# Order of the first loads, the queue of the layer-one words, PSUM banks and waiting rules in a planned attention and two-layer feed-forward kernel

## The chip, the cores and the metric

The kernel runs on one core of one Trainium2 chip. A core has five instruction streams: TensorE (PE, matrix products, with PEld for its weight loads), VectorE (DVE), ScalarE (ACT), GpSimd (POOL) and SyncE (SP, which here only issues DMAs). The metric is device microseconds of one execution, lower is better.

## The reference

A linear recurrence over 768 steps for 4 x 8 heads of size 40 makes a sequence of tokens, and two feed-forward layers follow on all 3072 tokens.

```python
for t in range(S):                       # B, H, S, D = 4, 8, 768, 40
    y[:, :, t] = einsum('bhd,bhde->bhe', rt, state)
    Sa = einsum('bhde,bhe->bhd', state, at)
    state = state * wt - Sa bt^T + vt kt^T
x = y.transpose(0, 2, 1, 3).reshape(3072, 320)
h = x @ w_in;   x = (h * tanh(softplus(h))) @ w_out      # layer one, d_ff 2048
h = x @ w_in2;  out = (h * cos(h)) @ w_out2              # layer two, d_ff 2048
```

## The kernel before

**Attention.** The 768 steps are 24 chunks of 32, and the heads are two halves, so there are 48 steps `g` (chunk `g // 2`, half `g % 2`). `pre(g)` loads a step's inputs into `IN` (two buffers, and a piece of `TMP` for `g = 1`), scans the decay (L559 to L565), makes `AM` and `KB` (L573, L579), multiplies them on TensorE (`g1`, L596), masks the product (L606) and stores it to `l_d`. `inverse` reads two steps' products back into `XM`, solves 28 small VectorE instructions one after the other (L668, L666), stores `t_d` and loads it as `TT`; `halves` (L705 to L713) ends the inverse. `chain(g)` carries the state: L776, L790, L822 or L799, L848, L874, L918 on TensorE, with evictions on ACT and VectorE between them (L389, L858, L885), and writes `Y` (L893). When four steps are done their `Y` goes to `x_d`.

**Feed-forward.** `layer1(blk)` takes one of 12 blocks of 256 tokens. It loads `XR`, splits it in a rounded part `XH` (ACT, L1032) and a rest `XL` (DVE, L1034), and runs eight groups: `h_tasks` (L977, 16 matmuls), two Mish activations (L1047, L1049), `GL` (L1052), `outs` (L958, 12 matmuls). A block can begin when the chain has made its four steps. `layer2` does the same with a cosine, mostly on blocks of 512 tokens (L992, L1008), after all of layer one's attention buffers are free (`switch`).

**Weights.** `prep` loads 64-bit words of 512 columns (`RW` or `RL` buffers), and turns each into a rounded part and a rest: Prelu on ACT (L458), a shift and an or on DVE (L463, L468), a copy `hi` on ACT or DVE (L389, L391), a subtraction `lo` on POOL (L497). Layer one's words are converted during the first chunks, layer two's after the chain has ended. Prelu and Mish are in different activation tables.

**The order.** Every piece of work is a `Task` of a `Plan`. `Plan.run` walks through modelled time: on each engine it picks the task that can start first, with small ties broken by `prio`, and so fixes the order of instructions on every engine when the kernel is built. Chain tasks have the lowest `prio` numbers (first), then `pre` and `inverse`, layer one's words, layer one, layer two. A DMA task is taken to land `lat` us after its issue (`DMA_LAT` is 3.0). Small matmuls use parts of the array (`MODE`); a group that would change TensorE from full to part use is held for up to `AGE` = 8 us, to go with others. PSUM has eight banks: four in ring `PA` for the attention, two in `PH` and two in `PO` for the feed-forward.

The built program has one thing that is not in the Python text: the landing of each DMA is told by one of eight semaphores `DMAHW0` to `DMAHW7`, which the DMAs of all queues are given in turn. A DMA therefore waits on its queue until the one that last had its semaphore has landed.

## Time and profile before

| | |
|---|---|
| three runs | 1154.07, 1154.3, 1161.89 us (median 1154.3) |
| profiled execution | 1154.66 us |
| span of its trace | 1153.0 us, so 1.66 us lie outside the trace |
| busy: PE, PEld | 1025.2 us (89%), 935.7 us (81%) |
| busy: DVE, ACT, POOL | 805.2 us (70%), 599.3 us (52%), 221.5 us (19%) |

The span is that from the first to the last instruction. Busy shares are averages over very different stages: the attention with layer one's words, attention with layer one, layer one with layer two's words, and layer two. The stages are to be read apart.

### The profile page before, as it was taken

The page shows a single profiled execution, that of the slowest core. Times are in us where ns is not written, and L with a number is a line of the kernel's source. Part 1 is how long each engine was busy: PE and PEld are TensorE (multiplying, and loading weights), DVE is VectorE, ACT ScalarE, POOL GpSimd, SP SyncE. Part 2 cuts the span into 40 slices and gives each one's busy share as a digit, 9 for nine tenths or more (in the row PEclk, how much of TensorE's full clock was granted, in tenths as well). Part 3 has the DMA queues.
Part 4 walks back from the last instruction along what each step waited for, and adds up shares of the span by engine and source line. Part 5 has one row for each costly group of instructions (what it writes and reads, how often), then busy time and mean ns, then how long its engine had stood idle before and what let it go on. Part 6 is the DMA issues. An engine that isn't in the chain of part 4 may idle for free.

```text
span 1153.0 us, 36365 instructions
## 1 busy us (share of the span) xinstructions
PE 1025.2 (89%) x14888; PEld 935.7 (81%) x14888; DVE 805.2 (70%) x2212; ACT 599.3 (52%) x1403; POOL 221.5 (19%) x278
## 2 busy tenths in 40 slices
PE   2265889999999999999998998889999999999997
PEld 1254678888888888989888898778999898999996
DVE  8898987897879779687677833535755655555553
ACT  3344595556455366455454646996533534343433
POOL 4223110000000000000000000333433333333333
PEclk9999999999999999989899999999999999999999
DMA  8553752554444436353552424342120101010001
GB/s 228 148 155 102 199 149 82 142 143 120 126 129 122 122 87 191 74 146 76 148 152 72 126 68 142 115 149 62 42 61 14 34 18 37 15 31 7 16 8 24
DMA packets 109366, 111.88 MB, mean 97 GB/s; under 512 B 64144, under 2 KB 88720, under 8 KB 109200
## 3 DMA queue, kind: packets, MB, share of 16 engines
q1 hardware_dynamic: 109200, 109.57, 35.0%
q8 instruction: 117, 1.92, 0.7%
q14 instruction: 49, 0.40, 0.1%
HBM read 91.43 MB, written 18.09 MB: 95 GB/s over the span
## 4 chain that ended last, share of the span: by engine, by line
PE 53%; DVE 14%; ACT 7%; issue 5%; DMA 3%; SPq 2%; POOL 0%; DVEq 0%; ACTq 0%; POOLq 0%
PE bank L992 12%; PE bank L1008 11%; PE bank L958 11%; PE bank L977 9%; DVE SV L885 2%; DVE FR L858 1%; DVE AM L606 1%; DVE XM L666 1%; DVE XT L668 1%; ACT L1047 1%; ACT L458 1%; PE bank L874 1%; PE bank L596 1%; DVE Y L893 1%; DVE GL L1052 1%
## 5 line engine op out<-in xcount | busy, mean ns | idle before, releaser
L1135 POOL TENSOR_TENSOR GL<-H,GH 128x512 fp32r<-128x512 f32 x96 | 124.2, 1298 | 215.4 <-ACT GH L1133 212.2
L389 ACT ACTIVATE FL<-bank 40x160 f32<-40x160 f32 (+1 forms) x375 | 101.2, 295 | 117.4 <-PE bank L629 60.0
L1126 ACT ACTIVATE T<-T,half_pi 128x512 f32<-128x512 f32 x96 | 69.4, 723 | 120.4 <-DVE T L1123 120.3
L1119 DVE TENSOR_SCALAR T<-bank 128x512 f32<-128x512 f32 x96 | 66.2, 689 | 91.2 <-PE bank L992 81.0
L1052 DVE TENSOR_TENSOR GL<-H,GH 128x512 fp32r<-128x512 f32 x96 | 66.8, 696 | 64.6 <-ACT GH L1049 63.7
L587 POOL MEMSET AM<- 64x256 f32 x96 | 29.3, 305 | 400.6 <-issue 308.4
L977 PE MATMUL bank<-XH,wih 128*128 128x256 f32 x448 | 95.0, 294 | 0.8 <-ACT GH L1049 0.8
L1128 DVE TENSOR_TENSOR H<-bank,T 128x512 f32<-128x512 f32 x96 | 65.9, 687 | 42.2 <-ACT T L1126 41.4
L1047 ACT ACTIVATE H<-bank 128x512 f32<-128x512 f32 x96 | 57.4, 598 | 68.1 <-PE bank L977 67.1
L1133 ACT ACTIVATE GH<-H 128x512 fp32r<-128x512 f32 x96 | 60.6, 632 | 60.4 <-DVE H L1128 57.3
L977 PE MATMUL bank<-XL,wih 128*128 128x256 f32 x448 | 89.7, 282 | 0.0
L977 PE MATMUL bank<-XH,wil 128*128 128x256 f32 x448 | 89.2, 281 | 0.0
L596 PE MATMUL bank<-AM,KB 104*64 104x64 f32 x768 | 37.5, 248 | 48.9 <-DVE KB L579 41.9
L668 DVE TENSOR_TENSOR XT<-XM 64x26 f32<-64x26 f32 (+6 forms) x336 | 67.9, 202 | 16.2 <-DMA XM<-l_d 8.1
L874 PE MATMUL bank<-FR,FL 104*64 104x72 f32 x1536 | 64.4, 241 | 12.9 <-issue 6.1
L666 DVE TENSOR_TENSOR XM<-XM,XT 64x26 f32<-64x26 f32 (+6 forms) x336 | 68.9, 205 | 8.2
L596 PEld LDWEIGHTS bank<-AM,KB 104*64 104x64 f32 x768 | 31.0, 157 | 52.7 <-issue 44.2
L874 PEld LDWEIGHTS bank<-FR,FL 104*64 104x64 f32 x1536 | 57.0, 147 | 19.7 <-issue 6.5
L977 PEld LDWEIGHTS bank<-XH,wih 128*128 128x128 f32 x448 | 69.9, 191 | 3.2 <-ACT GH L1049 1.3
L958 PE MATMUL bank<-woh1a,GH 128*128 128x320 f32 x192 | 65.3, 340 | 7.9 <-ACT GH L1049 7.8
L606 DVE TENSOR_TENSOR AM<-bank,maskG 64x128 f32<-64x128 f32 x192 | 55.1, 287 | 24.7 <-PE bank L596 18.6
L977 PEld LDWEIGHTS bank<-XL,wih 128*128 128x128 f32 x448 | 69.6, 192 | 0.0
(168 smaller groups left out, 2985.9 us busy)
## 6 DMA issues: line engine op xcount, KB each, us to landing
VR<-in_vR_dram SPq DMA_DIRECT2D x96, 160.0 KB
IN<-in_inT_dram SPq DMA_DIRECT2D x94, 161.4 KB
FR<-in_rI_dram SPq DMA_DIRECT2D x48, 180.0 KB
...
```

Of the source, the lines that this page charges most:

```text
L389: A.activation(o, i, AF.Copy)
L596: PE.matmul(gp[c0:c0 + 64, q // 2], kb()[:, q].rearrange("p a t -> p (a t)"), am()[0:104, :, q], start=True, stop=True)
L666: V.tensor_tensor(out=b[:, 0:i, i + 1:16], in0=b[:, 0:i, i + 1:16], in1=tv, op=ALU.add)
L668: V.tensor_tensor(out=tv, in0=bc(b[:, i:i + 1, i + 1:16], (2 * n, i, w)), in1=bc(b[:, 0:i, i:i + 1], (2 * n, i, w)), op=ALU.mult)
L874: PE.matmul(fp[64 * p:64 * p + 64, qp], fl()[0:104, n * D:n * D + 64], fr()[:, n], start=True, stop=True)
L958: PE.matmul(o, l[:, f, tsl], r, start=(first and f == 0 and i == 0), stop=(last and f == 1 and i == 2))
L977: PE.matmul(hp[:, f], pss[i][0], pss[i][1], start=(i == 0), stop=(i == 7))
L992: PE.matmul(bank[P.at((key, "h"))][:, 0:512], pss[i][0], pss[i][1], start=(i == 0), stop=(i == 7))
L1008: PE.matmul(o, l, r, start=(ft == 0 and i == 0), stop=(ft == NFF - 1 and i == 2))
L1052: gl = P.add(GLE, (dve(512),), lambda eng, Hv=Hv, key=key: EN[eng].tensor_tensor(out=GL_t[P.at((key, "gl"))], in0=Hv(), in1=GH_t[P.at((key ...
L1126: c = P.add("ACT", act(512, False, 1), lambda f=f, Tv=Tv: A.activation(Tv(f), Tv(f), AF.Sin, scale=-TWO_PI, bias=half_pi), preds=[b], aset ...
L1135: gl = P.add("POOL", pool(512), lambda f=f, Hv=Hv, key=key: G.tensor_tensor(out=GL_t[P.at((key, "gl"))], in0=Hv(f), in1=GH_t[P.at((key, "g ...
```

## The change

Five things change, all in what the planner is told or in who does a task.

1. `pre(g)` is entered before `load_step(g)`, the input loads of the first three steps get the lowest `prio` of all, and the rows 40 to 63 of `IN` are no longer set by DVE (`setup_in`, six memsets) but loaded from a new input `pad`. Loads of `r` and `v` wait for the scan of their step (first chunk) or for the loads of two steps before.
2. Layer one's words are issued on ScalarE's queue instead of SP's, with at most 3 instead of 6 under way (`AHEAD_W`).
3. DMA tasks carry their size `kb`: on SP's queue they land one after the other at 180 kB a microsecond plus 2 us, on ScalarE's after their own size at 100 kB a microsecond plus 2 us.
4. All eight PSUM banks are in `PA` until the first block's four steps are done; then two each are given to `PH` and `PO`.
5. `AGE` is 3 instead of 8; the `hi` copies of layer two's words go to DVE alone (`HIE2`); the second batch's inverse gets the priority pull that the first had (`PULL_INV`); the split of the first block's input has a chain's priority (`prx`).

```diff
-PULL, PULL_INV, PULL_CH = 0.3, -5000.0, -1e6
+PULL, PULL_INV, PULL_CH = 0.3, -4980.0, -1e6
...
-AGE = 8.0
+AGE = 3.0
 WAIT = 8.0
 SP_SAFE = 1.0
+RATE, RATE2, LAND = 180.0, 100.0, 2.0
+ACT_SAFE = 2.0
...
-                        st = max(st, (h[0][0] if n == 1 else sorted(h)[n - 1][0]) + (SP_SAFE if e == "SP" else 0.0))
+                        st = max(st, (h[0][0] if n == 1 else sorted(h)[n - 1][0]) + (SP_SAFE if e == "SP" else ACT_SAFE if ring in ("RW", "RL") else 0.0))
...
+            lat = t.lat
+            if t.kb and e == "ACT":
+                lat = t.kb / RATE2 + LAND
+            elif t.kb:
+                queue = max(queue, free[e]) + t.kb / RATE
+                lat = queue + LAND - free[e]
...
-                 ("PA", 4), ("PH", 2), ("PO", 2)):
+                 ("PA", 8), ("PH", 0), ("PO", 0)):
         P.ring(n, k)
-
-    def setup_in(i):
-        t = IN1 if i == 2 else IN_t[i]
-        V.memset(t[32:64, 0:768], 0.0)
-        V.memset(t[32:64, 768:], 1.0)
...
-    AHEAD_W = 6
+    AHEAD_W = 3
...
-    HIE2, HID2 = ("ACT", "DVE"), (act(512, False), 0.34)
+    HIE2, HID2 = ("DVE",), (0.34,)
...
-            t0 = P.add("SP", 0.5, lambda raw=raw, src=src: SP.dma_start(raw().rearrange("p n w -> p (n w)"), src),
+            t0 = P.add(*(("ACT", 0.4) if layer == 1 else ("SP", 0.5)), lambda raw=raw, src=src, q=A if layer == 1 else SP:
+                       q.dma_start(raw().rearrange("p n w -> p (n w)"), src),
...
             SP.dma_start(t[64:104], ins["inT"][hf, c, 1])
-
-        t_ld = fifo("ld", P.add("SP", 1.0, ld, preds=[S_IN[2]] if g == 1 else S_IN[0:2], acq=[] if g == 1 else [("IN", k("IN"))], lat=DMA_LAT + 1.5, prio=pr))
+            if g < 3:
+                SP.dma_start(t[40:64], ins["pad"])
+
+        t_ld = P.add("SP", 1.0, ld, acq=[] if g == 1 else [("IN", k("IN"))], kb=330, prio=pr if g > 3 else g - 1e6)
...
+        held = list(io[g - 2]) if c else [scanT[g]]
...
+        prx = -9.955e3 if blk == 0 else pr0
...
     for g in range(TOT):
+        pre(g)
         load_step(g)
-        pre(g)
...
+    for i in range(4):
+        P.add("SP", 0.0, lambda i=i: P.grow("PH" if i < 2 else "PO", [P.at(("bank", i))], P.time),
+              preds=ytask[0], acq=[("PA", ("bank", i))], lat=0.0, prio=-2e4)
```

The planned order changes on every engine. In what follows a name such as `AM1_202` is buffer 1 of `AM`; lines above L340 or so are a few numbers higher in the changed file (L453 is L456, L656 is L663, L977 is L985).

On SP, before: from the input of step 3 to the load that brings the first two products back for the first inverse (`XM<-l_d0`).

```order
L553 DMA IN0_192<-in_inT_dram 40x1033 [waits DMAHW5_49]
L554 DMA IN0_192<-in_inT_dram 40x1033 [waits DMAHW6_49]
L619 DMA l_d0_93<-AM1_202 32x8x32 [waits DMAHW7_49,DVE_49,Pool_49]
L620 DMA l_d0_93<-AM1_202 32x8x32 [waits DMAHW0_49,DVE_49,Pool_49]
L453 DMA TMP_172<-in_w_in_dram 128x1024 [waits DMAHW1_49]
L453 DMA TMP_172<-in_w_in_dram 128x1024 [waits DMAHW2_49,Activation_49]
L453 DMA TMP_172<-in_w_out_dram 128x1024 [waits DMAHW3_49,DVE_49,Activation_49]
L656 DMA XM_224<-l_d0_93 32x512 [waits DMAHW7_49,DMAHW4_49,DMAHW0_49]
```

On SP, now, the same place: the second step's product to the same load.

```order
L626 DMA l_d0_93<-AM1_202 32x8x32 [waits DMAHW7_49,DVE_49,Pool_49]
L627 DMA l_d0_93<-AM1_202 32x8x32 [waits DMAHW0_49,DVE_49,Pool_49]
L556 DMA IN1_193<-in_inT_dram 40x1033 [waits DMAHW1_49,DVE_49]
L557 DMA IN1_193<-in_inT_dram 40x1033 [waits DMAHW2_49]
L626 DMA l_d1_94<-AM2_203 32x8x32 [waits DMAHW4_49,DVE_49,Pool_49]
L627 DMA l_d1_94<-AM2_203 32x8x32 [waits DMAHW5_49,DVE_49,Pool_49]
L663 DMA XM_224<-l_d0_93 32x512 [waits DMAHW7_49,DMAHW6_49,DMAHW0_49]
```

Three words have left the place ahead of that load, and the input of step 4 stands there instead; its wait for `DMAHW1` is for a word that ScalarE issues, the last row of the next piece.

On ACT, now: the evictions of the first steps (`FL`), with the words' DMAs and conversions between them.

```order
L392 ACTIVATE FL1_209<-bank3_147 64x160 x3
L392 ACTIVATE wih1_164<-H0_177 128x512 [waits DVE_49]
L392 ACTIVATE FL2_210<-bank5_149 64x160 [waits PE_49]
L392 ACTIVATE FL2_210<-bank5_149 64x160 x3
L461 ACTIVATE H0_177<-TMP_172 128x512 [waits DMAHW0_49,Pool_49]
L456 DMA TMP_172<-in_w_out_dram 128x1024 [waits DMAHW1_49]
```

The word's DMA, which stood on SP before, now stands on ACT behind a conversion that waits for a landing and for POOL.

On TensorE, before: the last groups ahead of layer one's first matmul (`XH`, L977); `FL4` is of step 4.

```order
L596 MATMUL bank1_145<-AM2_203,KB0_217 64x64 x8
L629 MATMUL bank2_146<-ident_173,KB0_217 128x104 x4
L848 MATMUL bank3_147<-VR0_222 64x64 x8
L822 MATMUL bank0_144<-ident_173,ZS0_230 40x128 x4
L874 MATMUL bank1_145<-FR0_220,FL4_212 64x72 x8
L874 MATMUL bank2_146<-FR0_220,FL4_212 64x72 x8
L977 MATMUL bank4_148<-XH0_185,wih1_164 128x256 x2
```

On TensorE, now, the same place (L603 is L596, L985 is L977).

```order
L784 MATMUL bank6_150<-SV1_219,AM5_206 32x40 x16
L603 MATMUL bank2_146<-AM1_202,KB0_217 64x64 x8
L636 MATMUL bank4_148<-ident_173,KB0_217 128x104 x4
L985 MATMUL bank0_144<-XH0_185,wih1_164 128x256 x2
L985 MATMUL bank0_144<-XH0_185,wil1_165 128x256 x2
L985 MATMUL bank0_144<-XH0_185,wix1_166 128x256
```

Step 4's chain work has moved behind the first layer-one matmul, and the groups of the next steps' products stand directly ahead of it.

On ACT, before: the first of layer two's words (`AU<-RA`) among layer one's Mish activations (`H`, `GH`).

```order
L458 ACT_TABLE_LOAD
L458 ACTIVATE AU0_11623<-RA0_11620 128x512
L458 ACTIVATE AU1_11624<-RA1_11621 128x512
L1047 ACT_TABLE_LOAD
L1047 ACTIVATE H1_178<-bank0_144 128x512
L1049 ACTIVATE GH0_180<-bank0_144 128x512
L389 ACTIVATE wih2_11595<-AU0_11623 128x512
```

On ACT, now, the same place.

```order
L461 ACT_TABLE_LOAD
L461 ACTIVATE AU0_11412<-RA0_11409 128x512
L1056 ACT_TABLE_LOAD
L1056 ACTIVATE H1_178<-bank2_146 128x512
L1058 ACTIVATE GH0_180<-bank2_146 128x512
L1056 ACTIVATE H2_179<-bank4_148 128x512
L1058 ACTIVATE GH1_181<-bank4_148 128x512
```

The copies `wih2<-AU` have left ACT, and more Mish activations stand between two loads of a table.

## Rows read from the trace of the kernel before

**Rows 1.** Windows: length, then busy us of PE, PEld, DVE, ACT, POOL.

```profile
0.00:134.50 134.50, 61.02 (x1376) 50.95 (x1376) 119.39 (x345) 56.80 (x155) 38.36 (x78) 1.00 0.59 163
134.50:186.80 52.30, 46.62 (x850) 42.66 (x849) 43.56 (x141) 39.60 (x90) 10.50 (x20) 0.97 0.52 145
186.80:254.90 68.10, 64.14 (x1454) 57.51 (x1454) 59.77 (x206) 38.19 (x114) 3.67 (x12) 0.97 0.51 133
254.90:706.20 451.30, 428.17 (x8623) 392.40 (x8622) 339.39 (x1137) 237.32 (x681) 15.27 (x50) 0.98 0.43 114
706.20:790.00 83.80, 70.00 (x478) 65.15 (x477) 35.45 (x58) 73.65 (x104) 23.19 (x17) 0.96 0.42 133
790.00:1145.50 355.50, 355.19 (x2118) 326.99 (x2116) 207.60 (x330) 152.91 (x259) 130.49 (x101) 1.00 0.11 28
```

**Rows 2.** Timeline (start, length): XL of three blocks, and first matmuls of them.

```profile
133.17 0.95 DVE L1034 TENSOR_TENSOR XL<-XR,XH 128x768 fp32r<-128x768 f32 x1
134.54 0.79 PE L977 MATMUL bank<-XH,wih 128*128 128x256 f32 x2
...
181.29 0.96 DVE L1034 TENSOR_TENSOR XL<-XR,XH 128x768 fp32r<-128x768 f32 x1
...
186.84 0.39 PE L977 MATMUL bank<-XH,wih 128*128 128x256 f32 x2
...
239.37 0.96 DVE L1034 TENSOR_TENSOR XL<-XR,XH 128x768 fp32r<-128x768 f32 x1
...
254.93 0.39 PE L977 MATMUL bank<-XH,wih 128*128 128x256 f32 x2
255.16 0.39 PE L977 MATMUL bank<-XH,wil 128*128 128x256 f32 x2
```

**Rows 3.** Lines of DVE in 0 to 134 us: count, busy us, mean ns.

```profile
L666 DVE TENSOR_TENSOR XM<-XM,XT 64x14 f32<-64x14 f32 (+6 forms) x56 | 14.0, 250 | 1.3
L668 DVE TENSOR_TENSOR XT<-XM 64x14 f32<-64x14 f32 (+6 forms) x56 | 13.9, 248 | 3.8 <-DMA XM<-l_d 2.5
L468 DVE SCALAR_TENSOR_TENSOR H<-TMP,H 128x512 uint32<-128x512 uint32 x17 | 11.5, 678 | 0.1
...
L579 DVE TENSOR_TENSOR KB<-IN,RP 104x256 f32<-104x256 f32 x20 | 8.3, 416 | 0.2
...
L342 DVE MEMSET IN<- 32x768 f32 x2 | 1.4, 698 | 1.1 <-PEq L1318 1.0
```

**Rows 4.** Timeline of SP's DMA issues and DVE, 12 to 41 us.

```profile
12.03 0.71 DVE L559 TENSOR_TENSOR_SCAN PE<-IN,D 104x264 f32<-104x264 f32 x1
...
28.95 2.16 SPq L453 DMA_DIRECT2D TMP<-in_w_in_dram  x2
...
31.91 0.80 SPq L656 DMA_DIRECT2D XM<-l_d  x2
...
40.01 0.17 DVE L668 TENSOR_TENSOR XT<-XM 64x14 f32<-64x14 f32 x1 [2.54 <-DMA XM<-l_d]
```

**Rows 5.** DMA queues in 0 to 40 us.

```profile
DMA packets 4162, 8.96 MB, mean 224 GB/s; under 512 B 1856, under 2 KB 2112, under 8 KB 4160
```

**Rows 6.** Timeline of TensorE at a change from full to part use.

```profile
309.51 0.31 PE L958 MATMUL bank<-wol1b,GH 128*128 128x320 f32 x1
309.65 0.30 PE L958 MATMUL bank<-woh1b,GL 128*128 128x320 f32 x1
309.89 0.75 PE L705 MATMUL bank<-TA,TT 16*32 16x32 f32 x64
```

**Rows 7.** Lines of ACT in 710 to 790 us: count, busy us, mean ns.

```profile
L458 ACT ACT_TABLE_LOAD x12 | 15.4, 1283 | 0.2
L1047 ACT ACT_TABLE_LOAD x11 | 14.1, 1283 | 0.2
...
L389 ACT ACTIVATE wih<-AU 128x512 fp32r<-128x512 f32 x8 | 5.0, 631 | 1.5 <-DVE AU L468 1.4
```

**Rows 8.** Lines of PE in 710 to 790 us: busy us, mean ns, idle before.

```profile
L958 PE MATMUL bank<-woh1a,GH 128*128 128x320 f32 x32 | 11.0, 343 | 7.9 <-ACT GH L1049 7.8
```

More of the change, by code (lines that the diff above doesn't have):

```diff
@@ L50, with __init__ @@
 SLACK = {"PE": 0.02, "DVE": 0.02, "ACT": 0.02, "POOL": 0.2, "SP": 0.02}
-PULL, PULL_INV, PULL_CH = 0.3, -5000.0, -1e6
+PULL, PULL_INV, PULL_CH = 0.3, -4980.0, -1e6
 class Task:
-    __slots__ = ("eng", "dur", "fn", "preds", "acq", "rel", "aset", "lat", "prio", "end", "n_wait", "succ", "ready", "cols", "engs", "takes", "name", "durs", "bias", "ffn", "port", "mode", "soft", "pull", "mate")
-    def __init__(self, eng, dur, fn, preds=(), acq=(), rel=(), aset=None, lat=None, prio=0.0, cols=0.0, bias=BIAS, port=False):
-        self.bias = bias
+    __slots__ = ("eng", "dur", "fn", "preds", "acq", "rel", "aset", "lat", "prio", "end", "n_wait", "succ", "ready", "cols", "engs", "takes", "name", "durs", "bias", "ffn", "port", "mode", "soft", "pull", "mate", "kb")
+    def __init__(self, eng, dur, fn, preds=(), acq=(), rel=(), aset=None, lat=None, prio=0.0, cols=0.0, bias=BIAS, port=False, kb=0.0):
+        self.bias, self.kb = bias, kb
         self.ffn = cols > 0 and prio >= 0
@@ L135, in run @@
         done = 0
-        port_free = 0.0
+        port_free = queue = 0.0
         recent = []
@@ L229, in run @@
                 port_free = free[e]
-            t.end = free[e] + (0.2 if t.lat is None else t.lat)
+            lat = t.lat
[4 more added lines that the diff above has]
+                lat = queue + LAND - free[e]
+            t.end = free[e] + (0.2 if lat is None else lat)
             for key in t.rel:
@@ L238, in run @@
                 for x in u.engs:
-                    u.ready[x] = max(u.ready[x], free[e] + (HOP.get((e, x), 0.15) if t.lat is None else t.lat))
+                    u.ready[x] = max(u.ready[x], free[e] + (HOP.get((e, x), 0.15) if lat is None else lat))
                 u.n_wait -= 1
@@ L562, in pre @@
         t_sc = fifo("scan", P.add("DVE", 0.62, scan, preds=[t_ld, S_D], acq=[("PE", k("PE"))], prio=pr, port=True))
+        scanT[g] = t_sc
         def rscan():
@@ L620, in ldm @@
             SP.dma_start(ld_v[ci, 1], am()[32:64, 1])
-        ldma[g] = P.add("SP", 1.0, ldm, preds=t_gl, lat=DMA_LAT, prio=pr)
+        ldma[g] = P.add("SP", 1.0, ldm, preds=t_gl, kb=128, prio=pr)
         fl = lambda: FL_t[P.at(k("FL"))]
@@ L656, in ld @@
                 SP.dma_start(part(h), dr(l_d, h))
-        t = P.add("SP", 1.0, ld, preds=[ldma[g0 + i] for i in range(cnt)] + [S_X], acq=[("X", ("X", bt))], lat=DMA_LAT, prio=pr)
+        t = P.add("SP", 1.0, ld, preds=[ldma[g0 + i] for i in range(cnt)] + [S_X], acq=[("X", ("X", bt))], kb=140, prio=pr)
         def step(i, add):
@@ L741, in f3 @@
                 V.memset(sv[64:104, 1], 0.0)
[L743 to L745 removed]
+        t3 = P.add("SP", 1.0, f3, preds=[S_V] + held, acq=[("SV", k("SV"), 3 if c else 1)], kb=106, prio=pr)
+        t1 = P.add("SP", 1.0, f1, preds=[S_V] + held, acq=[("FR", k("FR"))], kb=331, prio=pr)
+        t2 = P.add("SP", 1.0, f2, preds=[S_V] + held, acq=[("VR", k("VR"))], kb=328, prio=pr)
         io[g] = (t1, t2, t3)
@@ L938, in yst @@
                 SP.dma_start(xv[1], yv[64:104])
-            ytask.setdefault(yb, []).append(P.add("SP", 1.0, yst, preds=yevs, rel=[ykey], lat=DMA_LAT, prio=pr))
+            ytask.setdefault(yb, []).append(P.add("SP", 1.0, yst, preds=yevs, rel=[ykey], kb=164, prio=pr))
     x2st = {}
@@ L1154, in store @@
                     SP.dma_start(out[r0:r0 + 64], OB_t[P.at(ok)][64 * i:64 * i + 64])
-            P.add("SP", 1.0, store, preds=[o], rel=[ok], lat=DMA_LAT, prio=pr0)
-    S_IN = [P.add("DVE", 1.1, lambda i=i: setup_in(i), prio=-1e6) for i in range(3)]
+            P.add("SP", 1.0, store, preds=[o], rel=[ok], kb=164, prio=pr0)
     S_D = P.add("DVE", 0.7, setup_d, prio=-9.5e5)
@@ L1210, in switch @@
             P.grow(r, range(len(STG[r])), P.time)
-        P.grow("PH", [0, 1], P.time)
-        P.grow("PO", [2, 3], P.time)
+        left = [i for _, i in P.rings["PA"]]
+        P.grow("PH", left[0:2], P.time)
+        P.grow("PO", left[2:4], P.time)
     def half2():
@@ L1265, in layouts @@
                           wp.reshape(NPART, NCH, 2, D, NQ * (C + 1)), wp[..., 0, :1]], axis=-1)
+    pad = np.zeros((64 - D, inT.shape[-1]), np.float32)
+    pad[:, 3 * NQ * C:] = 1.0
     def nlay(x):
@@ L1304, in layouts @@
     return {
-        "inT": inT, "rI": units(rI), "vF": units(vF), "vS": vS, "vR": vR,
+        "inT": inT, "pad": pad, "rI": units(rI), "vF": units(vF), "vS": vS, "vR": vR,
         "w_in": win_lay(w_in), "w_out": wout_lay(inputs["moe_w_out"]),
```

22 lines of the change are left out of this document (8 added, 14 removed).

## The prediction

> **What bounds the kernel now.** I read the windows first, since the averages of the page hide five different stages [rows 1]. Up to 134.5 us DVE is busy 119.4 us and PE 61.0: TensorE waits for what VectorE makes (scans, products, inverses, words). From 134.5 to 254.9 DVE still has 103.3 of 120.4 us, while PE has risen to 110.8. From 254.9 to 706.2 PE is busy 428.2 of 451.3 us and DVE 339.4: TensorE sets the pace. From 706.2 to 790 the chain is over, layer one goes on beside the conversion of layer two's words, and ACT is the full engine: 73.7 of 83.8 us, PE 70.0. From 790 on PE is never idle until 1145.5, and 7.5 us of output follow. So there are two places where TensorE waits and time can be had, the start and the stretch behind the chain. What is gained on another engine between 254.9 and 706.2 is worth little.
>
> Second I read where the first three blocks of layer one begin [rows 2]. `XL` of the first is ready at 134.1 and TensorE takes it at once. `XL` of the second starts at 181.3, its first matmul at 186.8. `XL` of the third is done at 240.3, but TensorE comes to it only at 254.9: there the bound has passed from DVE to PE. The third block is therefore the point at which I compare the two orders.
>
> **The change part by part. The first 250 us.** The order of DVE gives, by counting: ahead of the first `XL` stand 343 instructions before and 274 now, ahead of the second 472 and 517, ahead of the third 640 and 642. The 69 that leave the first stretch are the six memsets of `setup_in`, 17 instructions of the words, 27 of one inverse, and 19 of the steps' preparation and chain; the kinds cost 0.70 (the three longer memsets), 0.68 (an or of the words), 0.25 (an inverse's piece) and 0.42 us (a `KB`) [rows 3]. Priced by the mean of the stretch, 119.39 / 345 = 0.346 us [rows 1], they are 24 us. The 45 more ahead of the second `XL`, at 43.56 / 141 = 0.309 us [rows 1], are 14 us. The two more ahead of the third are 0.6 us. So the change brings the first block forward and pays it back before the third; what it removes for good on DVE is the memsets, about 3 us, which these counts already contain.
>
> To this come waits of DVE that the trace of before can't show. The first scan starts at 12.0 us now [rows 4]; the inputs that lead the queue let it start earlier, perhaps by 3. But the DMAs of the first 40 us move 8.96 MB at 224 GB/s [rows 5], so what leads pushes something else back. The first inverse started at 40.0 after 2.5 us of waiting for `XM<-l_d`, issued at 31.9, behind words issued from 28.95 [rows 4]. In the new order those words are gone from ahead of it, which speaks for an earlier inverse by up to 5 us. Instead the load of step 4 stands there, which shares its completion semaphore with a word that ACT issues, and that word stands on ACT behind a conversion that waits for POOL. SP's in-order queue then holds back the loads for the first inverse until the word has landed. I bound the cost of this from -5 us (words gone, no wait) to +12 us (two inverses, each 6 us late; 8.1 us is what the load took from issue to use at 40.0 [rows 4]) and take +4, nearer to the first end, because fewer words compete for the saturated DMA engines.
>
> Then the first `XL` starts at 133.2 - 24 + 4 = 113, and layer one about 1.4 us later (134.54 against 133.17 [rows 2]), 20 us earlier than before. The second `XL` starts at 181.3 + 14 + 4 = 199 and its block at about 202. Between the second and third block TensorE did 128 matmuls of L977, 96 of L958 and 660 small ones in the 68.1 us from 186.8 to 254.9. L977 follows itself by 0.115 us (255.16 - 254.93 for two) [rows 2], L958 by 0.147 (309.51 to 309.65) [rows 6]: 14.7 + 14.1 us, so the small ones took 39.3, or 0.06 each. Now 128, 84 and 320 stand there: 14.7 + 12.3 + 19.1 = 46 us. So the third block begins at 202 + 46 = 248, where `XL` (239.4 + 0.6 + 4 = 244) has just been made, 7 us earlier than 254.9. Up to that point 48 small matmuls fewer have been done, 2.9 us. Net **-4 us**, with bounds of -13 (TensorE takes the third block as soon as `XL` is made without the waits) and +5 (waits at 12).
>
> The DMA issues of layer one's words leave SP, which nothing waits for as an engine, and take some 0.4 us each on ACT; ACT is busy 56.8 of the first 134.5 us [rows 1], so this hides as long as no issue waits. Three `pad` loads of 99 kB are 0.3 MB, 1.3 us of the rate in [rows 5], inside the bound above. Eight banks instead of four cost nothing and I give them nothing: the waits of the first stretch are for DVE.
>
> **Changes of mode.** The order of TensorE goes from full to part use 161 times instead of 145 and back 162 instead of 146; changes among part uses fall from 100 to 90. One entry took 0.24 us from start to start where the matmul before took 0.14 [rows 6], so 0.1 us; 22 changes more are **+2 us**, from 0 (hidden in waits) to 4.
>
> **The middle.** When the chain ends, 112 matmuls of L977 and 78 of L958 more are still to do than before: 24 us of layer one are left for later, and the chain ends that much earlier. DVE's 339.4 us then fall into 427 instead of 451, 79% instead of 75%. Still not the bound; I add **+1 us** for more meetings, 0 to 8.
>
> **Layer two's words.** In 710 to 790 us ACT spends 29.5 us in 23 table loads, and its copies of `hi` take 0.63 us each [rows 7]; 20 of them stand in the order there, 12.6 us. They go to DVE, which is busy 35.5 of 83.8 us [rows 1], so it hides them. In the new order 22 Mish pairs instead of 16 share the stretch, with 27 table loads instead of 23. ACT's work becomes 73.7 - 12.6 + 4 x 1.28 + 6 x 1.2 + some 4 us for two more words and the outputs = 77 us, while TensorE's is 22 x (16 x 0.115 + 12 x 0.147) = 79 instead of 58. ACT no longer exceeds TensorE. PE's idle there, 83.8 - 70.0 = 13.8 us [rows 1], of which 7.9 stood before one line waiting for ACT's `GH` [rows 8], should fall to about 6: **-8 us**, bounds -14 and 0. If DVE did not hide the copies, conversions would end some 10 us later, and layer two is still far off.
>
> A table load shows 1283 ns here and 0.2 us of idle in front of twelve of them together [rows 7]. The Trainium skill (ScalarE: Activation LUTs, What ACT_TABLE_LOAD costs) gives the same 1283 ns, but adds a drain of about 1380 ns to every switch of sets. By the Trainium skill the four more would cost 10.6 us of ACT instead of 5.1 and the forecast would be some 5 us later; the rows show no such drain, so I price them by the row.
>
> **The sum.** 1154.66 - 4 + 2 + 1 - 8 = 1145.7 us, for an execution with 1.66 us outside the trace; the profiled execution is 0.4 us above the median of 1154.3, so I say 1145.5, 0.8% less.
>
> **Rivals.** (A) The start pays in full: TensorE begins layer one at about 110, 24 us earlier, and is fed from then on, because the second chunk's chain no longer waits for its inverse. The 140 small matmuls that are moved behind the start cost 8 us at 0.06, the modes 2, the words' stretch gives 10: 1154.7 - 24 + 8 + 2 - 10 = 1131. For it speaks that TensorE is idle 73 of the first 134.5 us; against it that the second and third `XL` have as much DVE work ahead as before or more.
>
> (B) Slower: the shared semaphores couple the two queues. Each word on ACT waits for a DMA of SP eight places back, and SP for words of ACT, so that evictions stand behind DMA issues and loads behind evictions. What the planner takes to be 0.4 us of issue becomes a wait of several us for ten words, and both first inverses come late. Third block 21 us later than forecast, 269: 1167. It decides from the point where the first inverse starts later than about 46 us. For it speak the order's rows and the saturated DMA [rows 5]; against it that before, too, words and loads stood in one queue with the same semaphores. The Trainium skill (DMA: Bandwidth & Descriptors, Issuing engines are not separate DMA queues) says that DMAs of ScalarE and SyncE run on the same 16 engines and interleave, so that a second queue saves issue time alone. The trace, with one queue in use, does not show two sharing.
>
> (C) The words' stretch gives nothing: Mish, Prelu and two banks still take turns, and four more table loads eat the freed copies: 1145.7 + 8 = 1154.
>
> **How the numbers follow.** Forecast 0.47, A 0.30, B 0.13, C 0.10. One per cent of 1154.3 is 11.5 us, about what a measurement of this kernel tells from no change: faster means below 1142.8, slower above 1165.8. The forecast's own spread, 1138 to 1153, puts some 0.07 below 1142.8: faster 0.37. Of B a fifth stays below 1165.8: slower 0.11. The rest is 0.52. The range of 1128 to 1163 leaves out a third of A and three quarters of B, 2 in 10.
>
> **What would show it.** Right: the first L985 near 114 us and the third block near 248; the first inverse near 40; PE idle between 115 and 200; fewer PE waits for `GH` behind the chain; 38 table loads instead of 34 in all. Wrong: a third block before 240 (A) or after 260 (B), DVE waiting long for `XM` or `IN`, ACT idle before a DMA issue, or PE idle of over 10 us behind the chain (C).

## The result, and the profile after

The changed kernel is slower: the median of its eight runs is 1166.41 us (1161.93 to 1171.01) against 1154.18 us of eight runs of the kernel before, a ratio of 1.0104 with a 95% interval of 1.0074 to 1.0135. I had forecast 1145.5 us and a range up to 1163. The profiled execution took 1165.52 us, its span is 1163.8.

The windows of the changed kernel, cut at the first matmul of the first three blocks (121.0, 226.5, 275.2), of the eleventh block (733.8), and of layer two (798.3). Columns as in [rows 1].

```profile
0.00:121.00 121.00, 45.64 (x1109) 39.59 (x1109) 87.92 (x274) 41.85 (x119) 29.18 (x67) 0.91 0.56 158
121.00:226.50 105.50, 78.80 (x1677) 70.26 (x1678) 89.56 (x271) 67.77 (x169) 22.55 (x35) 0.78 0.49 128
226.50:275.20 48.70, 45.52 (x814) 42.11 (x813) 37.19 (x138) 22.20 (x63) 1.23 (x4) 0.96 0.40 102
275.20:733.80 458.60, 432.84 (x8702) 393.04 (x8701) 358.81 (x1159) 251.63 (x701) 22.89 (x59) 0.99 0.46 124
733.80:798.30 64.50, 61.43 (x456) 58.95 (x455) 42.48 (x65) 51.91 (x71) 20.44 (x15) 1.00 0.43 128
798.30:1163.80 365.50, 357.56 (x2140) 329.83 (x2138) 205.95 (x332) 152.23 (x258) 128.00 (x99) 1.00 0.11 26
```

These are the cuts of [rows 1] except for the last: layer two's first matmul stood at 787.1 us before, and [rows 1] cut at 790.0. The stretch that compares with the one from 733.8 to 798.3 is this one of the kernel before:

```profile
706.20:787.10 80.90, 67.10 (x457) 62.26 (x456) 34.32 (x56) 70.96 (x99) 23.19 (x17) 0.96 0.43 138
```

Length less PE busy is TensorE's idle time. Up to the third block it is 75.4 + 26.7 + 3.2 = 105.3 us, against 73.5 + 5.7 + 4.0 = 83.2 in [rows 1]. In the middle it is 25.8 against 23.1. In the stretch behind the chain it is 3.1 against 13.8. So 22 us are lost at the start, 3 in the middle and 11 come back behind the chain, 14 more in all; TensorE's busy time is 3.4 us shorter (1021.8 against 1025.2), which leaves the 10.8 us by which the span is longer. By landmarks the third block is 20.3 us late (275.2 against 254.9), the eleventh 27.6 (733.8 against 706.2), layer two 11.2 (798.3 against 787.1), the end 10.8.

The timeline shows the three starts that answer to [rows 2]: the `XL` and the first matmul of each block (the third block's `XL` is there 18 us before its matmul).

```profile
120.98 0.80 PE L985 MATMUL bank<-XH,wih 128*128 128x256 f32 x2 [10.92 <-ACT XH L1041]
...
217.06 0.96 DVE L1043 TENSOR_TENSOR XL<-XR,XH 128x768 fp32r<-128x768 f32 x1
...
226.45 0.40 PE L985 MATMUL bank<-XH,wih 128*128 128x256 f32 x2
...
257.21 0.94 DVE L1043 TENSOR_TENSOR XL<-XR,XH 128x768 fp32r<-128x768 f32 x1
```

VectorE's work ahead of the first block did shrink, from 119.4 us (345 instructions) to 87.9 (274), but it waits. The waits of DVE in the first 130 us, and its timeline where these waits end:

```profile
DVE PE L564 <- DMA IN<-in_inT_dram: 11.2, 2, 6.6
DVE PE L564 <- DMA IN<-in_pad_dram: 7.8, 1, 7.8
DVE XT L675 <- DMA XM<-l_d: 3.1, 2, 1.6
```

```profile
13.47 0.71 DVE L564 TENSOR_TENSOR_SCAN PE<-IN,D 104x264 f32<-104x264 f32 x1 [7.76 <-DMA IN<-in_pad_dram]
...
41.30 0.71 DVE L564 TENSOR_TENSOR_SCAN PE<-IN,D 104x264 f32<-104x264 f32 x1 [4.55 <-DMA IN<-in_inT_dram]
...
44.99 0.17 DVE L675 TENSOR_TENSOR XT<-XM 64x14 f32<-64x14 f32 x1 [1.44 <-DMA XM<-l_d]
...
114.51 0.71 DVE L564 TENSOR_TENSOR_SCAN PE<-IN,D 104x264 f32<-104x264 f32 x1 [6.60 <-DMA IN<-in_inT_dram]
```

Before, no scan waited for `IN`; one inverse waited 2.5 us [rows 4]. Why the inputs come late is seen on SP's queue, in its longest waits (first 130 us: sum, times, longest) and its timeline.

```profile
SPq L735 <- DMA TMP<-in_w_in_dram: 10.3, 1, 10.3
SPq L626 <- DVE AM L613: 8.2, 4, 3.3
SPq L557 <- DMA TMP<-in_w_out_dram: 8.0, 1, 8.0
SPq L556 <- DVE XT L675: 7.0, 1, 7.0
SPq L556 <- DMA TMP<-in_w_out_dram: 5.6, 1, 5.6
```

```profile
20.20 0.30 SPq L556 DMA_DIRECT2D IN<-in_inT_dram  x1
28.56 0.29 SPq L557 DMA_DIRECT2D IN<-in_inT_dram  x1
...
37.20 0.30 SPq L556 DMA_DIRECT2D IN<-in_inT_dram  x1
...
94.07 0.28 SPq L741 DMA_DIRECT2D VR<-in_vR_dram  x1
104.76 0.28 SPq L735 DMA_DIRECT2D FR<-in_rI_dram  x1
...
109.14 0.37 SPq L556 DMA_DIRECT2D IN<-in_inT_dram  x1
```

An input load (L556, L557) has nothing to do with a word in `TMP`; what it waits for is the semaphore that this word's landing holds. All such waits for words add up to 46.1 us in the first 130; before they were 5.1. At 20.5 us SP stops between the two halves of one input, until a word lands at 28.5. That word was issued on ACT's queue at 25.01, as ACT's timeline shows:

```profile
13.23 0.35 ACTq L456 DMA_DIRECT2D TMP<-in_w_out_dram  x1
22.07 0.99 ACT L392 ACTIVATE FL<-bank 64x160 f32<-64x160 f32 x4 [8.18 <-PE bank L636]
25.01 0.34 ACTq L456 DMA_DIRECT2D TMP<-in_w_out_dram  x1
...
33.48 0.33 ACTq L456 DMA_DIRECT2D TMP<-in_w_out_dram  x1
```

The word of 25.01 stands behind an eviction that waited 8.2 us for TensorE, which waited for VectorE, which waited for its first input. So SP's load waits for ScalarE, and ScalarE for the loads' own consumers. This first stop alone made no scan wait: the scan of that input began at 31.47 us with no idle time before it. The next ones did. SP stood for 5.6 us (the last row of its waits) until 37.2, for a word that ACT issued at 33.48, and the scan at 41.30 waits for the input that then left at 37.20. The scan at 114.51 waits for the input issued at 109.14, after SP had stood for 10.3 us until 104.7. The DMA engines were not full meanwhile: the line that answers to [rows 5], for 0 to 40 us, has 6.82 MB instead of 8.96, and the queues' share of the 16 engines was 59% instead of 79%.

```profile
DMA packets 3370, 6.82 MB, mean 171 GB/s; under 512 B 1694, under 2 KB 1822, under 8 KB 3368
```

The first wait, 7.8 us for `pad`, is partly something else: in the first 13.5 us the words on ACT's queue (q10) moved more bytes than the inputs that lead SP's (q1); the columns are packets, MB and share of the 16 engines.

```profile
q10 hardware_dynamic: 432, 1.57, 40.2%
q1 hardware_dynamic: 369, 1.19, 30.0%
```

The Trainium skill (DMA: Bandwidth & Descriptors, Issuing engines are not separate DMA queues) says that DMAs of several issuing engines run on the same 16 engines and interleave. The two lines agree: both queues move bytes in the same stretch, and their shares add up to 70.2%.

Behind the chain the change did what it was meant to. ACT's lines from 735 to 798 us (answer to [rows 7]), and PE's line that answers to [rows 8]:

```profile
L461 ACT ACT_TABLE_LOAD x9 | 11.5, 1283 | 0.2
L1056 ACT ACT_TABLE_LOAD x9 | 11.5, 1283 | 0.2
```

```profile
L966 PE MATMUL bank<-woh1a,GH 128*128 128x320 f32 x32 | 10.1, 315 | 1.1 <-ACT GH L1058 1.0
```

No copies `wih<-AU` are left on ACT, and PE's idle at this line, nearly all of it for `GH`, has gone from 7.9 to 1.1 us. Part of the words now lies ahead of the window from 733.8: ACT's first table load for them is at 711.7 us, where it was at 710.8. From there to layer two's first matmul TensorE is idle for 4.0 of 86.6 us with 614 matmuls, where it was idle for 13.8 of 76.3 with 423. Idle ahead of nine loads of a table together is again 0.2 us, so the drain that the Trainium skill adds (ScalarE: Activation LUTs, What ACT_TABLE_LOAD costs) does not show here either.

### The profile page after: what moved, and what is told of

It reads as the page before. It is cut to its first block, busy times and chain, and to the rows that moved or that the text cites. A ratio compares the mean times of both kernels' runs of the same rounds, so it can differ in the third digit from the quotient of the medians.

```text
span 1163.8 us, 36363 instructions
## 1 busy us (share of the span) xinstructions
PE 1021.8 (88%) x14888; PEld 933.8 (80%) x14888; DVE 821.9 (71%) x2234; ACT 587.6 (50%) x1379; POOL 224.3 (19%) x278
## 4 chain that ended last, share of the span: by engine, by line
PE 62%; DVE 21%; issue 5%; DMA 5%; ACT 5%; SPq 1%; POOL 0%; DVEq 0%; ACTq 0%; POOLq 0%
PE bank L966 13%; PE bank L1000 12%; PE bank L985 12%; PE bank L1016 11%; PE bank L882 3%; DVE XM L673 3%; DVE SV L893 3%; DVE XT L675 3%; DVE AM L613 2%; PE bank L856 2%; PE bank L798 2%; DVE AM L580 1%; DVE GL L1061 1%; DVE KB L586 1%; PE bank L603 1%
## 5 line engine op out<-in xcount | busy, mean ns | idle before, releaser
L392 ACT ACTIVATE FL<-bank 64x160 f32<-64x160 f32 (+1 forms) x376 | 101.5, 295 | 127.7 <-PE bank L636 68.2
L985 PE MATMUL bank<-XH,wih 128*128 128x256 f32 x448 | 95.4, 295 | 14.2 <-ACT XH L1041 10.9
L1061 DVE TENSOR_TENSOR GL<-H,GH 128x512 fp32r<-128x512 f32 x96 | 68.7, 719 | 49.1 <-ACT GH L1058 47.7
L985 PE MATMUL bank<-XL,wih 128*128 128x256 f32 x448 | 90.2, 283 | 0.0
L985 PE MATMUL bank<-XH,wil 128*128 128x256 f32 x448 | 90.2, 283 | 0.0
L985 PEld LDWEIGHTS bank<-XH,wih 128*128 128x128 f32 x448 | 71.1, 194 | 16.3 <-ACT XH L1041 11.2
L603 PE MATMUL bank<-AM,KB 104*64 104x64 f32 x768 | 37.0, 246 | 49.1 <-DVE KB L586 41.0
L675 DVE TENSOR_TENSOR XT<-XM 64x14 f32<-64x14 f32 (+6 forms) x336 | 67.8, 202 | 14.0 <-DMA XM<-l_d 5.8
L603 PEld LDWEIGHTS bank<-AM,KB 104*64 104x64 f32 x768 | 30.6, 155 | 55.5 <-issue 42.3
L673 DVE TENSOR_TENSOR XM<-XM,XT 64x14 f32<-64x14 f32 (+6 forms) x336 | 67.7, 201 | 8.5
L985 PEld LDWEIGHTS bank<-XL,wih 128*128 128x128 f32 x448 | 70.3, 193 | 0.0
L985 PEld LDWEIGHTS bank<-XH,wil 128*128 128x128 f32 x448 | 70.2, 194 | 0.0
```

The costliest lines, as they stand in the source:

```text
L392: A.activation(o, i, AF.Copy)
L603: PE.matmul(gp[c0:c0 + 64, q // 2], kb()[:, q].rearrange("p a t -> p (a t)"), am()[0:104, :, q], start=True, stop=True)
L673: V.tensor_tensor(out=b[:, 0:i, i + 1:16], in0=b[:, 0:i, i + 1:16], in1=tv, op=ALU.add)
L675: V.tensor_tensor(out=tv, in0=bc(b[:, i:i + 1, i + 1:16], (2 * n, i, w)), in1=bc(b[:, 0:i, i:i + 1], (2 * n, i, w)), op=ALU.mult)
L985: PE.matmul(hp[:, f], pss[i][0], pss[i][1], start=(i == 0), stop=(i == 7))
L1061: gl = P.add(GLE, (dve(512),), lambda eng, Hv=Hv, key=key: EN[eng].tensor_tensor(out=GL_t[P.at((key, "gl"))], in0=Hv(), in1=GH_t[P.at((key ...
```

## The experiments

Theory 1: the landing semaphores, given in turn over two queues, couple SP's loads to ScalarE's stream. Theory 2: the words only take DMA bandwidth from the inputs. Theory 3: the order itself lacks work to cover the loads. One table first: median, median of the kernel before measured beside it, starts of the first three blocks, TensorE's idle up to the third (window length less PE busy), and SP's waits for words (in `TMP` or `RL`) in 130 us (not summed where a dash stands). Blocks and idle times are of one profiled execution each.

| kernel | us | before | blocks 1, 2, 3 | idle | SP for words |
|---|---|---|---|---|---|
| before | 1154.18 | | 134.5, 186.8, 254.9 | 83 | 5.1 |
| changed | 1166.41 | 1154.18 | 121.0, 226.5, 275.2 | 105 | 46.1 |
| a_q_sp | 1147.62 | 1154.93 | 102.7, 210.4, 259.1 | 88 | 9.3 |
| a_q_pool | 1152.02 | 1154.93 | 102.1, 213.2, 261.9 | 85 | 0 |
| b_words_act | 1167.71 | 1154.93 | 136.1, 204.8, 272.5 | 96 | 23.8 |
| b_hi_dve | 1143.70 | 1154.93 | 134.7, 186.5, 254.5 | 82 | - |
| b_hi_age3 | 1142.64 | 1153.28 | 134.8, 199.1, 264.8 | 83 | - |
| b_hi_banks8 | 1155.71 | 1153.28 | 162.6, 213.7, 264.6 | 86 | - |
| b_hi_lead | 1164.85 | 1153.28 | 121.0, 188.6, 263.8 | 86 | 5.1 |
| a_words_sp | 1156.53 | 1153.28 | 142.0, 217.0, 271.9 | 93 | 4.4 |
| a_sp_hi_both | 1161.17 | 1155.25 | 104.1, 216.0, 264.6 | 89 | - |
| a_sp_inv | 1141.37 | 1155.25 | 113.8, 190.6, 250.1 | 82 | 13.7 |
| a_sp_fill | 1157.28 | 1155.25 | 106.6, 218.5, 267.1 | 82 | - |
| a_act_inv | 1165.74 | 1151.45 | 131.1, 213.6, 273.2 | 106 | 47.7 |

**a_q_sp.** The changed kernel, its order kept, words on SP's queue.

```diff
-... q=A if layer == 1 else SP:
+... q=SP:
```

> The changed kernel with its planned order kept, and one thing undone: layer one's words are issued on SP's queue, at the places where ScalarE issued them. PE and DVE have the same rows in the same order. Theory 1 (coupling): in the changed kernel SP's input loads wait for semaphores that words on ScalarE's queue hold, 46 us of SP waits for TMP in the first 130 us against 5 before. With one queue that waits in order, these waits should fall below 15 us, DVE's waits for IN from 18.9 us to below 9, and the time to about 1153. Theory 2 (bytes): words and inputs share the same 16 DMA engines whatever queue they are on; inputs come about as late as now, the time stays within 1161 to 1168. Theory 3 (the order): too little work is left on DVE to cover the loads, the waits for IN stay near 18 us, 1163 to 1168.

Measured: 1147.62 us, ratio to before 0.9939 (0.9906 to 0.9972), 18.8 us less than the changed kernel. The windows up to the third block, and the first scan:

```profile
0.00:102.70 102.70, 45.62 (x1109) 39.59 (x1109) 87.64 (x272) 41.89 (x119) 29.20 (x67) 0.93 0.65 183
102.70:210.40 107.70, 81.11 (x1676) 71.94 (x1677) 89.63 (x272) 67.59 (x169) 22.31 (x35) 0.77 0.48 129
210.40:259.10 48.70, 44.08 (x814) 40.55 (x813) 37.19 (x138) 22.26 (x63) 1.22 (x4) 1.00 0.41 101
```

```profile
7.69 0.71 DVE L564 TENSOR_TENSOR_SCAN PE<-IN,D 104x264 f32<-104x264 f32 x1 [1.98 <-DMA IN<-in_pad_dram]
```

With the same instructions in the same order on PE and DVE, TensorE's idle ahead of the first block falls from 75.4 to 57.1 us; the next two stretches stay as they were. Theory 3 falls. Theory 1 gave 1153, the loss was larger. Of the 18.3 us, 5.8 are the first scan (7.69 instead of 13.47). The `pad` that it waits for left SP at 4.63 us in the changed kernel and at 2.76 here, and the scan followed 8.8 and 4.9 us later: 1.9 us lie ahead of the issue and 3.9 behind it. Behind it the bytes of theory 2 are the likely cause, and no run shows them alone. The rest fits the later waits of DVE: for `IN` 11.2 us there and none here, for `XM` 3.1 and 1.3.

**a_q_pool.** The same with GpSimd's queue.

```diff
-... q=A if layer == 1 else SP:
+... q=G if layer == 1 else SP:
```

> The changed kernel, same order on PE and DVE, words issued on GpSimd's queue, whose landings have semaphores of their own, so that no load of SP and no word wait for one another's semaphores. The bytes still go through the same 16 DMA engines at the same time. Theory 1 (coupling): SP no longer waits for TMP, DVE's waits for IN fall below 8 us, first block near 111, third near 260, time about 1150; GpSimd pays some 1 us an issue, which delays its subtractions little. Theory 2 (bytes): IN waits stay at 15 to 19 us, 1162 to 1168. Theory 3 (the order): also 1162 to 1168.

Measured: 1152.02 us, 0.997 (0.9946 to 0.9993); SP waits for no word, DVE's wait for `IN` is 1.7 us. Two queues did no such harm where SP waits for no landing of the other, so the later waits are theory 1's. As far as the traces show, the turn of eight semaphores is thus one of SP's and ScalarE's queues, and GpSimd's landings have others. An issue took GpSimd 0.56 us (27 of them 15.2), not the 1 us that I expected. The first words left it only at 7.0 us, so this run does not tell the first scan's 5.8 us apart.

**b_words_act.** The kernel before, words planned and issued on ScalarE.

```diff
-            t0 = P.add("SP", 0.5, lambda raw=raw, src=src: SP.dma_start(...
+            t0 = P.add(*(("ACT", 0.4) if layer == 1 else ("SP", 0.5)), lambda raw=raw, src=src, q=A if layer == 1 else SP:
+                       q.dma_start(...
```

> The kernel before with one thing of the change alone: layer one's words are issued on ScalarE's queue (still up to six under way, planned at 3 plus 1.5 us). Theory 1 (coupling): SP's loads begin to wait for words, 20 to 50 us of SP waits for TMP in the first 130 us, DVE's waits for IN or XM rise by 8 to 20 us, time 1160 to 1172. Theory 2 (bytes): within 3 us of before, 1152 to 1157, since the same bytes move at the same time. Theory 3 (the order): 1152 to 1157.

Measured: 1167.71 us, 1.0102 (1.0065 to 1.0139), inside theory 1's range, but only in part for its reason. SP waits 23.8 us for words (17.5 for those in `TMP`, 6.3 for those in `RL`), the third block is 17.6 us late and TensorE's idle up to it 12 us longer. But DVE's waits for `IN` or `XM`, expected to rise by 8 to 20 us, are 1.4 us in the first 130; it waits for `TT` instead (6.2 us in the first 230). And 14 us more idle stand in layer two (21.4 against 7.8), with a cause that no run here shows.

**a_act_inv.** The changed kernel with the second inverse pulled as before.

```diff
-PULL, PULL_INV, PULL_CH = 0.3, -4980.0, -1e6
+PULL, PULL_INV, PULL_CH = 0.3, -5000.0, -1e6
```

> The changed kernel with the pull of the second inverse as before (PULL_INV -5000) and nothing else undone: layer one's words are on ScalarE's queue. Order of PE and DVE as in the kernel of 1141.4 us, which issues the words on SP. Theory 1 (coupling, whatever the order): SP waits 25 us or more for words in the first 130 us, DVE 10 to 20 us for IN or XM, TensorE's idle up to the third block 95 us or more against 82.4, time 1153 to 1162. Rival (the coupling cost much because the second inverse stood where it did): idle up to the third block below 88 us, 1141 to 1147.

**a_sp_inv.** The same order on PE and DVE, words on SP: both diffs, this one and that of a_q_sp.

> The changed kernel with words on SP's queue, and the pull of the second inverse as before (PULL_INV -5000). First XL behind 299 DVE instructions instead of 274, second 491 instead of 517, third 665 instead of 642. Theory P (DVE pays the early first block back before the second): first block 8 us later than 102.7, second XL 8 us earlier than 200, TensorE's idle between the first two blocks falls from 26.6 us to 12 to 18 and that ahead of the first rises from 57 by as much, so that the idle up to the third block stays at 82 to 90 us and the time at 1142 to 1152. Rival (the pull is what costs the start): idle up to the third block falls to 75 us or less, below 1140.

Measured: 1165.74 us, 1.0104 (1.0066 to 1.0142), against 1141.37 us, 0.9897 (0.9848 to 0.9946). The windows up to the third block, first of a_act_inv, then of a_sp_inv:

```profile
0.00:131.10 131.10, 47.15 (x1172) 40.27 (x1172) 100.88 (x300) 46.11 (x126) 31.00 (x70) 0.85 0.54 156
131.10:213.60 82.50, 65.75 (x1256) 58.43 (x1249) 66.36 (x203) 57.54 (x141) 16.73 (x28) 0.87 0.45 125
213.60:273.20 59.60, 54.50 (x1195) 48.80 (x1194) 50.79 (x170) 31.96 (x93) 3.67 (x12) 1.00 0.49 132
```

```profile
0.00:113.80 113.80, 47.18 (x1172) 40.52 (x1173) 101.04 (x300) 46.30 (x126) 31.06 (x70) 0.83 0.63 179
113.80:190.60 76.80, 65.82 (x1255) 58.90 (x1249) 66.99 (x204) 57.39 (x141) 16.79 (x28) 0.88 0.48 134
190.60:250.10 59.50, 54.69 (x1193) 49.07 (x1193) 50.75 (x169) 31.96 (x93) 3.68 (x12) 0.99 0.49 133
```

A second order shows the same: DVE does 101 us of work in 131 us or in 114, and the queue alone is worth 24 us. Theory 1 has its waits (47.7 us of SP, 19.0 of DVE) and its idle (106); the time went above its 1162. As for the pull, theory P is right on the shift (first block 11 us later than in a_q_sp, idle between the first two blocks 11.0 instead of 26.6), but the idle up to the third also fell by 6, and the time by 6. The two intervals overlap, and 6 us are about what one execution can differ from another (a_sp_hi_both), so what the place of the second inverse costs is not settled.

**a_words_sp.** The changed kernel with the words also planned on SP (its `P.add` as in before, with `kb=n`).

> The changed kernel with the words planned and issued on SP's queue, so that the order is made for one queue; all other parts as changed. The order now has 352 DVE instructions ahead of the first XL (274 with the words on ScalarE), 520 and 641 ahead of the second and third. Theory 1 (coupling): no waits of SP for words beyond 15 us, DVE waits for IN below 6 us, time 1142 to 1150, near the 1147.6 of the kept order on one queue. Rival (the order made with the words on ScalarE was itself the gain of the start): third block at 265 or more, 1153 to 1160.

Measured: 1156.53 us, 1.0014 (0.9993 to 1.0035). SP waits 4.4 us for words, and yet the first block starts at 142.0 and the third at 271.9: the rival's numbers. So the coupling is not all of the start. An order made for two queues and run on one is 9 us better than the order that the planner makes for one.

**b_hi_dve.** The kernel before with the `hi` copies on DVE.

```diff
-    HIE2, HID2 = ("ACT", "DVE"), (act(512, False), 0.34)
+    HIE2, HID2 = ("DVE",), (0.34,)
```

> The kernel before with one thing of the change alone: the copies hi of layer two's words go to DVE and not to ScalarE. The order is the same up to the middle of the chain's time. Theory W (the copies bound the stretch): the stretch behind the chain becomes 12 to 17 us shorter, ScalarE's busy time in it falls by about 12 us, 1138 to 1143. Rival (what shortened the stretch in the changed kernel was that more of layer one's Mish pairs were left beside the words): a gain of at most 5 us, 1149 to 1155.

Measured: 1143.70 us, 0.9889 (0.9852 to 0.9926). The stretch behind the chain:

```profile
703.90:772.50 68.60, 61.75 (x457) 58.76 (x456) 48.11 (x76) 57.14 (x77) 24.99 (x17) 1.00 0.50 161
```

It is 68.6 us long instead of 80.9 (706.2 to 787.1), ACT's busy time 57.1 instead of 71.0, TensorE's idle 6.9 instead of 13.8. Theory W holds, one line alone gives 11 us.

**a_sp_hi_both.** That line undone in a_q_sp.

> The changed kernel with words on SP's queue at the planned places (1147.6 us), and the hi copies of layer two's words undone: ScalarE or DVE makes them, as before. The order is the same up to row 2422 of TensorE's 4414. Theory W (the copies on ScalarE bound the stretch behind the chain): TensorE's idle in that stretch goes from 3.1 us back to 10 to 14, time 1155 to 1162. Rival (the stretch is short because more Mish pairs share it): idle stays below 6 us, 1146 to 1151.

Measured: 1161.17 us, 1.0052 (1.0026 to 1.0078). The stretch is 75.0 us instead of 64.5, TensorE's idle in it 9.4 (a little below what W expected) instead of 3.1, most of it at the lines that wait for `GH` (the one shown, and `woh1b` with 3.8 us):

```profile
723.90:798.90 75.00, 65.58 (x457) 62.21 (x456) 31.78 (x50) 63.08 (x91) 19.28 (x15) 0.95 0.37 114
```

```profile
L966 PE MATMUL bank<-woh1a,GH 128*128 128x320 f32 x32 | 10.8, 336 | 4.3 <-ACT GH L1058 4.3
```

Theory W again. The third block of this execution is 5.5 us later than that of a_q_sp, with the same order up to there: so much one profiled execution can differ from another.

**b_hi_age3.** b_hi_dve with the shorter wait for company.

```diff
-AGE = 8.0
+AGE = 3.0
```

> The kernel before, with the hi copies on DVE (1143.7 us so far) and the shorter wait of TensorE's groups for company (AGE 3 instead of 8) as the one part added. The third XL has 695 DVE instructions ahead instead of 640, the first 343 as before. Theory M1 (shorter waits cost mode changes and stand against layer one): the stretch from the third block to the eleventh grows from 449 to 455 us or more, time 1149 to 1156. Theory M2 (neutral: what is done earlier is missing later): 1140 to 1147.

Measured: 1142.64 us, 0.9894 (0.9859 to 0.9929): M2. From the third to the eleventh block it takes 451.7 us (449.4 in b_hi_dve). The third block is 10.3 us later than in b_hi_dve, at the same idle (83 against 82), and the end is not: 3966 matmuls instead of 3681 lie ahead of it. A late block is thus a loss only where no more work was done before it (3600 in the changed kernel, 3680 in the kernel before).

**b_hi_banks8.** b_hi_dve with eight banks in `PA` until the first block.

```diff
-                 ("PA", 4), ("PH", 2), ("PO", 2)):
+                 ("PA", 8), ("PH", 0), ("PO", 0)):
...
+    for i in range(4):
+        P.add("SP", 0.0, lambda i=i: P.grow("PH" if i < 2 else "PO", [P.at(("bank", i))], P.time),
+              preds=ytask[0], acq=[("PA", ("bank", i))], lat=0.0, prio=-2e4)
...
```

> The kernel before, with the hi copies on DVE, and all eight banks in the attention's ring until the first block's steps are done. The order moves the first XL behind 450 DVE instructions instead of 343, the second behind 498 instead of 472. Theory N (banks bound nothing, the start is for DVE): the first block comes near 165, but the second near 195 and the third near 258, time 1142 to 1149. Rival (TensorE did useful layer-one work in the 30 us that are now given to the attention, and lacks it later): third block at 270 or more, 1155 or more.

Measured: 1155.71 us, 1.0025 (1.0002 to 1.0048), 12 us above b_hi_dve, as the rival said; the third block (264.6) lies between the two. What the banks are worth in the changed kernel, where `prx` brings the first block forward, no run shows.

**b_hi_lead.** b_hi_dve with the new order of the inputs.

```diff
-        load_step(g)
         pre(g)
+        load_step(g)
...
+            if g < 3:
+                SP.dma_start(t[40:64], ins["pad"])
...
-        t_ld = fifo("ld", P.add("SP", 1.0, ld, ... prio=pr))
+        t_ld = P.add("SP", 1.0, ld, ... prio=pr if g > 3 else g - 1e6)
...
+        held = list(io[g - 2]) if c else [scanT[g]]
...
```

> The kernel before, with the hi copies on DVE, and of the start only the new order of the inputs: input loads of the first steps lead, the rows 40 to 63 of IN are loaded from pad, loads of r and v are held back; the words stay on SP's queue and nothing waits for ScalarE. First XL behind 305 DVE instructions instead of 343, second 456 instead of 472, third 659 instead of 640. Theory 1 (only the coupling of the queues spoilt the start): DVE's waits for IN stay below 6 us, first block near 121, third near 255, time 1138 to 1146. Theory 3 (leading inputs and held loads themselves make DVE wait): waits for IN above 12 us, third block above 262, 1150 to 1158.

Measured: 1164.85 us, 1.0088 (1.0055 to 1.0121), which neither theory gave. The start is theory 1's (first block 121.0, waits for `IN` 1.9 us), the second block is 2 us late. Then the order loses elsewhere: the stretch before the third block is 7 us longer than in b_hi_dve, and the one behind the first layer-two matmul 14:

```profile
778.70:1162.30 383.60, 364.18 (x2140) 333.29 (x2138) 219.90 (x360) 156.22 (x266) 140.59 (x108) 0.98 0.13 35
```

That has 19.4 us of idle against 10.1 in b_hi_dve, far from the place of the edit. A re-made order can bring such differences; why it did here is not shown.

**a_sp_fill.** a_q_sp with 128 useless matmuls in the first block.

```diff
+                    if part == 0 and xk == ("x1", 0):
+                        for _ in range(8):
+                            PE.matmul(hp[:, f], pss[0][0], pss[0][1], start=True, stop=True)
```

> The changed kernel with words on SP's queue, planned as it was, and 128 matmuls more in the first block: the first product of each of its 16 sums is made eight times more and thrown away, 14.7 us of TensorE at 0.115 us each. They lie in the 108 us between first and second block, where TensorE is idle 26.6 us and its granted clock is at the lower level in 65 of 97 us. Theory K (what TensorE has too much there is free, its idle there is waiting for DVE): second block within 3 us of 210.4, time 1146 to 1151. Theory L (the low clock costs the second block's start, and more work brings the higher level): second block 3 to 8 us earlier, 1140 to 1146. Theory M (TensorE bounds that stretch too): second block 10 to 25 us later, 1156 or more.

Measured: 1157.28 us, 1.002 (0.9997 to 1.0042), 9.7 more than a_q_sp. The stretch between the first two blocks is now

```profile
106.60:218.50 111.90, 91.25 (x1798) 82.87 (x1798) 89.03 (x271) 67.51 (x168) 21.34 (x34) 0.82 0.44 120
```

with the granted clock at 0.82 instead of 0.77 and the idle at 20.7 instead of 26.6. The second block is 8.1 us later, but 3.9 of them stand ahead of the first block, before the added matmuls, and so belong to this execution; the stretch itself is 4.2 us longer. K and L fall; M has the time, though not the place. By the medians 10 of the 14.7 added us come through, so TensorE's idle there is not all free room; where those beyond the 4.2 us of this stretch arise is not shown. The lower level of the clock held for some 50 of the 97 us, not for the 65 of my expectation: the clock is 0.68 from 103 to 150 us of a_q_sp and 0.80 from there to 200.1.

## Why the prediction was wrong

**The step that failed** is the wait of DVE for its loads, which I bounded "from -5 us (words gone, no wait) to +12 us" and took at "+4, nearer to the first end, because fewer words compete for the saturated DMA engines". It was some 20: in the first 130 us 19.0 for `IN` and 3.1 for `XM`, where before had 2.5 in all. A smaller part of that is the first scan, which I let start 3 us earlier and which started 1.4 us later (13.47 against 12.03). I had read the row in which SP's input load waits for a word of ScalarE, and priced only the inverse behind it. But the scans need that load themselves, and the same wait comes back at 94 to 105 us. Nor were the engines full, as "saturated" says: their share in the first 40 us was 79% before, and 59% now.

**The rival B** is what happened. Its price, third block at 269 and 1167 us, is close to 275.2 and 1166.4; that the time agrees to 1 us is luck, since the block came 6 us later and the words' stretch gave back 8 us more than forecast. Its sign was not: the first inverse started at 44.99, short of the 46 from which I let B decide, since the loss was spread over three scans. I gave B 0.13, with the argument that one queue had the same semaphores before. That argument is wrong: on one queue the holder of a semaphore has already been issued when the next user comes up; with two queues it may still stand behind an eviction.

**The rest of the start** is read in a_q_sp, where no coupling disturbs it. DVE lost 32 us of work ahead of the first block (I had 24), which came at 102.7 us and not at 114. Second `XL`: forecast 199, a_q_sp 200.08. But the second block came at 210.4 and not at 202, since TensorE was still at the first block's own matmuls (rows of a_q_sp):

```profile
199.96 0.31 PE L966 MATMUL bank<-woh1b,GL 128*128 128x320 f32 x1
...
204.14 0.28 PE L985 MATMUL bank<-XH,wix 128*128 128x256 f32 x1
```

From it to the third I had 46 us, and it took 48.7. The 660 and 320 small matmuls of that sum are some 1230 and 600 in the traces, in the same proportion, so the sum stands. Of the 27 us by which the third block missed 248, the queue accounts for 16 (a_q_sp). In a_sp_inv it came another 9 us earlier (250.1), in the fastest execution of four; how much of that is the pull is open. Rival A falls as well: TensorE did start early in a_q_sp, but was idle for 26.6 us before the second block.

**Modes and middle**: 451.3 plus 3 and the 48 small matmuls moved there (2.9 us) would be 457.2; it is 458.6. No run shows the 2 us for modes alone; AGE on top of b_hi_dve changed nothing that can be measured.

**The words' stretch** was mis-sized, -8 where it gave -16.4 (80.9 to 64.5 us); the mechanism was right (b_hi_dve, a_sp_hi_both), and rival C falls. I had kept 6 us of idle, 3.1 remained, or 4.0 from the words' first table load on; and TensorE's own busy time fell from 67.1 us to 61.4 with as many matmuls, at a granted clock of 1.00 instead of 0.96, which I had not counted. The 38 table loads are there. That a_q_sp, at 1147.62 us, is near the forecast of 1145.5 is therefore in part luck: its third block is 11 us later than 248, and its words' stretch is as short.

**Banks**: "cost nothing and I give them nothing" did not hold on the kernel before (b_hi_banks8).

**Open** is why re-made orders differ by some 10 us where the edit explains no wait (a_words_sp, b_hi_lead). Three versions are some 11 us faster than the kernel before: a_sp_inv (1141.37), b_hi_age3 (1142.64) and b_hi_dve (1143.70); their intervals do not rank them. a_q_sp gains 0.6% and a_q_pool 0.3%.
